# The first loads of an attention and gated-MLP kernel: heads on even and odd rows, whole weight units, and the masks' second part on another queue

## The chip, the cores and the metric

The kernel runs on one core of a Trainium2 chip. The metric is the time of one execution on the device, in microseconds (us). It was measured in three runs before the change: 947.91, 950.3 and 950.68 us, with a median of 950.3 us.

## The reference

The program computes windowed attention and puts its output through a gated MLP. All is in float32, for 8 batches, 8 heads, 576 positions and 64 numbers a head.

```
rel = pos[:, None] - pos[None, :]
mask = rel in [0, 32)                       for heads 0 to 3
mask = rel in [0, 128) and rel % 4 == 0     for heads 4 to 7
s = where(mask, q @ k.T / 8, -1e9)          # per batch and head
x = softmax(s) @ v                          # laid out as (4608 tokens, 512)
g = x @ w_gate                              # (512, 1536)
out = (silu(g) * (x @ w_val)) @ w_out       # (4608, 512)
```

A query sees 32 keys at most, in neighbouring positions or in every fourth one.

## The kernel before

**Packs.** Attention goes in packs: a pack holds two heads and up to a few groups of 128 queries. A group is four blocks of 32 queries, and each block sees 64 keys, so the scores of a block are a product of 32 columns of q with 64 columns of k. The first four packs (0 to 3) make the first 512 tokens of x and have four groups each; they have code of their own (`first_...`). Here the two heads of a pack are done by one product: the 128 rows hold head 0 in 64 of them and head 1 in the other 64, k stands twice, once for each head with zeros in the other head's rows, and so the product gives both heads side by side. The same goes for v.

**Weights.** The MLP's weights come in 24 units of 128 rows and 768 KB (two units for each of the 12 columns of 128 hidden numbers), as 64-bit floats. A unit is converted in five steps, named by the letters E, T, B, H, L: E (L242) on ScalarE, T on ScalarE (L259) or VectorE (L262), B (L269 or L272) on VectorE, H (the high part, L280) on ScalarE and L (the low part, L284) on GpSimd. Raw units stand in six places at first; a place comes free after step B, and then the next unit is loaded (`w_load`, L229 once `ready["w"]` is set).

**The order at the start.** All loads are issued on three queues: that of SyncE (SP), that of ScalarE (ACT), and that of GpSimd (POOL), each in order. `first_qk(m)` and `first_v(m)` load a pack's q and k, and v, as two halves: rows 0 to 63 (head 0) on the sync queue, rows 64 to 127 (head 1) on GpSimd's. The zeros that go with them are written by VectorE or GpSimd. A weight unit before `ready["w"]` also comes as two halves of 64 rows on these two queues (L231, L232). The masks' first part (128 x 640 of bf16) comes at the very start on ScalarE's queue, and the second part (128 x 320 of bf16, 80 KB), which pack 4 is the first to read, on the sync queue after five weight units (L607). A wait is there where a load's semaphore is still in use: there are eight for the loads that SP and ACT issue and eight for GpSimd's, given out in turn, so a load waits until the one eight before it has landed.

After the loads a written order follows, kept for TensorE, VectorE and ScalarE by `manual_schedule`:

```
for what in ("Q0 S0 Q1 Y2 S1 X0 Q2 X1 T0 S2 T1 K0 K1 A0 X2 N0 W0 T2 W1 A1 K2 W2 U0 Q3 H0 N1 W3 S3 U1 W4 A2 H1 "
             "L1 X3 N2 W0 T3 K3 W1 U2 A3 H2 L0 W2 W0 N3 W3 W4 W1 W0 U3 H3 L2 W1 W2 W0 L3 W2 W3 W1").split():
```

The digit is the pack. Q are the scores on TensorE (a mask product L372, then 32 small products L376), S the maximum and the subtraction on VectorE (L383, L384), X the exp on ScalarE (L440), T the transposition (L444) and K its copy (L450), A the product with v (L392), N the division by the sums on VectorE (L399 to L401), U the transposition back (L478), H and L the high and low part of x (L505 on ScalarE, L508 on VectorE). W0 to W4 are the steps E, T, B, H, L of the next weight unit.

**After it.** Then come the MLP's columns: `gv_mm` makes a column's gate and value products (bg and bv, L518, 12 products each), `act_tanh` (L527) and `dve_u` (L532) read the gate's bank, and only then can the next column's gate product write it; `out_mm` (L555) makes the output product of the column before. The attention of the later packs is put in between (`attend`): pack 4's mask products (L414) and scores (L420) come first. What isn't in the written order is placed by the scheduler, which may put a later product ahead of waiting ones, and each engine then keeps that order.

Of the kernel before, what the change touches and what calls it, by code (L numbers as in the profile page):

```python
# [12 lines left out]
I32 = mybir.dt.int32  # L13
# [5 lines left out]
P = 128  # L19
# [120 lines left out]
def attention_moe(ctx, tc, qkb, vb, w, masks, ident, out):  # L140
# [76 lines left out]
    def w_load():  # L217
        nonlocal loaded
        u = loaded
        n = u % 6 if u < NU - NLAST else (u + 2) % 4  # L220

        if u >= NU or raw_of.get(n, -1) >= done["B"]:
            return False
        raw_of[n] = u
        loaded += 1
        t = at(raw_at[n], 2 * WU, I32)
        src = w[u // 2, u % 2].bitcast(I32)
        if ready["w"]:
            last["w"] = nc.sync.dma_start(out=t, in_=src)  # L229
        else:  # L230
            nc.sync.dma_start(out=t[:D], in_=src[:D])  # L231
# [116 lines left out]

    def first_qk(m, zero):

        t, n = early["qk"](), pk(m).cols
        k = n - FN
        nc.sync.dma_start(out=t[:D, :n], in_=qkb[m, :D, :n])
        nc.gpsimd.dma_start(out=t[D:, k:k + n], in_=qkb[m, D:, :n])
        zero.memset(t[D:, :k], 0.0)
        zero.memset(t[:D, n:n + k], 0.0)
        st[m]["qk"] = t

    def first_v(m, zero):
# [5 lines left out]
        zero.memset(t[:D, 1], 0.0)  # L365
        st[m]["v"] = t.rearrange("p h (g c) -> p h g c", c=D + 1)

    def first_scores(m, bank):
        t, n = st[m]["qk"], pk(m).cols
        kk = t[:, :2 * n].rearrange("p (h c) -> p h c", h=2)  # L370
        mk = masks_of(m).rearrange("q (g k) -> q g k", g=FG).unsqueeze(2).broadcast_to([P, FG, 2, BK])
        nc.tensor.matmul(out=bank.rearrange("q (g h k) -> q g h k", g=FG, h=2), lhsT=ident16, rhs=mk, start=True,  # L372
                         stop=False, skip_group_check=True)
        for g, blocks in enumerate(pk(m).groups):
            for j, (_, _, _, q, k) in enumerate(blocks):
                nc.tensor.matmul(out=bank[BQ * j:BQ * j + BQ, P * g:P * g + P], lhsT=t[:, n - FN + q:n - FN + q + BQ],  # L376
                                 rhs=kk[:, :, k - FN:k - FN + BK], start=False, stop=g == FG - 1,
                                 skip_group_check=True)

    def first_shift(m, bank):  # L380
        mx, e = early["bm"](2 * FG), early["e"]()
        s, ev = [x.rearrange("q (g k) -> q g k", k=BK) for x in (bank, e)]
        nc.vector.reduce_max(out=mx, in_=s, axis=mybir.AxisListType.X)  # L383
        nc.vector.tensor_tensor(out=ev, in0=s, in1=mx.unsqueeze(2).broadcast_to([P, 2 * FG, BK]), op=ALU.subtract)  # L384
        st[m]["e"] = e.rearrange("q (g h k) -> q g h k", g=FG, h=2)

# [37 lines left out]
    def shift(m, two, pool, masked):  # L424
# [10 lines left out]
        nc.vector.tensor_tensor(out=ev, in0=s, in1=mx.unsqueeze(3).broadcast_to([P, 2, ng, BK]), op=ALU.subtract)  # L435
        st[m]["e"] = e

# [4 lines left out]
    def turn_e(m, bank):  # L442
        for g in range(pk(m).ng):
            nc.tensor.transpose(out=bank[:, P * g:P * g + P],  # L444
                                in_=st[m]["e"][:, g].rearrange("q h k -> q (h k)"), identity=idents[:, 0])

# [133 lines left out]
    near = P + 8 * BK  # L580
    nc.vector.memset(ones, 1.0)
    nc.vector.memset(some, 0.0)
    first_qk(0, nc.vector)
    nc.scalar.dma_start(out=consts[:, :near], in_=masks[:, :near])
    first_qk(1, nc.vector)
    nc.sync.dma_start(out=idents, in_=ident.rearrange("n p c -> p n c"))
    nc.scalar.activation(out=some, in_=some, func=AF.Exp)

    warm = ones.bitcast(BF16)
# [5 lines left out]

    idle(WARM)
    first_qk(2, nc.gpsimd)
    first_v(0, nc.vector)
    w_load()
    first_v(1, nc.gpsimd)  # L600
    first_qk(3, nc.gpsimd)
    first_v(2, nc.gpsimd)
    w_load()
    first_v(3, nc.gpsimd)
    for _ in range(3):
        w_load()
    nc.sync.dma_start(out=consts[:, near:], in_=masks[:, near:])  # L607
    while w_load():
        pass
    ready["w"] = True  # L610
# [10 lines left out]

    et = mybir.EngineType
    with tc.manual_schedule(engines={et.PE, et.DVE, et.Activation}):
        for what in ("Q0 S0 Q1 Y2 S1 X0 Q2 X1 T0 S2 T1 K0 K1 A0 X2 N0 W0 T2 W1 A1 K2 W2 U0 Q3 H0 N1 W3 S3 U1 W4 A2 H1 "
# [360 lines left out]
def layout(q, k, v, moe_w_gate, moe_w_val, moe_w_out):  # L985
# [3 lines left out]
    for m, pk in enumerate(PACKS):  # L989
        for i, (b, q0, n, qc, kc) in enumerate(x for g in pk.groups for x in g):  # L990
# [3 lines left out]
            for j in range(2):  # L994
                h, r = 2 * pk.pair + j, D * j
                nq = P * pk.ng
                x, y = (pk.cols - nq, -nq) if m < 4 and j == 0 else (0, 0)
                qkb[m, r:r + D, x + qc:x + qc + n] = q[b, h, qt].T
                qkb[m, r:r + D, y + kc + a:y + kc + e] = k[b, h, kt[a:e]].T
                vb[m, r + a:r + e, i, :D] = v[b, h, kt[a:e]]  # L1000
# [28 lines left out]
```

## Time and profile before

| | |
|---|---|
| median of three runs | 950.3 us |
| the profiled execution | 949.9 us |
| its span, first to last instruction | 948.1 us |
| TensorE busy | 926.8 us (98%) |
| VectorE, ScalarE, GpSimd busy | 641.0, 390.6, 256.8 us |
| mean granted TensorE clock | 0.996 |
| DMA, mean over the span | 217 GB/s |

The profiled execution is one of its own. Its span leaves out 1.8 us around the instructions. In the tables below a row of the chain of work is a start, a length and what the time went to; a row of the timeline is a start, a busy time, an engine, a line, an operation with what it writes and reads, and in brackets the idle time before it with what ended it; a row of windows has busy times of PE, PEld, DVE, ACT and POOL, then the granted clock, the DMA engines' busy share and their GB/s.

### The profile page before, as it was taken

To read this page: it belongs to the slowest core of one execution; us is meant where nothing else is said; L and a number is where in the kernel's file an instruction comes from. 1 tells how busy PE (TensorE), PEld (TensorE's weight loads), DVE (VectorE), ACT (ScalarE), POOL (GpSimd) and SP (SyncE) were. 2 spreads that over 40 slices of the span, in tenths; PEclk is the share of its full clock that TensorE was granted. 3 is DMA by queue.
4 is the path that set the end of the run, shared out by engine and by line. 5 is a ranking of instruction groups with operands and counts; after the bars stand their busy time and mean duration, and the time that the engine had idled before them with its cause. 6 is when DMAs were issued, how large, how long until landed. Compare 5 with 4: busy or idle time off the path is not lost.

```text
span 948.1 us, 20559 instructions
## 1 busy us (share of the span) xinstructions
PE 926.8 (98%) x8499; PEld 755.1 (80%) x8499; DVE 641.0 (68%) x1055; ACT 390.6 (41%) x664; POOL 256.8 (27%) x313
## 2 busy tenths in 40 slices
PE   7699999999999989999999999999999999999998
PEld 4587888878888878888888888888888888888886
DVE  5665755777687776466668975576689845656863
ACT  3566642333243333334335553334345623334351
POOL 7265441111111121122222211222222122333320
PEclk9899999999999999999999999999999999999999
DMA  9986522777676892576776768676766686556663
GB/s 256 315 285 215 169 82 92 241 239 253 218 267 236 270 331 80 177 236 216 222 240 219 244 227 273 204 250 201 245 209 199 203 264 198 187 192 200 190 212 109
DMA packets 75181, 205.45 MB, mean 217 GB/s; under 512 B 7760, under 2 KB 22352, under 8 KB 75088
## 3 DMA queue, kind: packets, MB, share of 16 engines
q0 software_dynamic: 28336, 103.66, 35.3%
q1 hardware_dynamic: 34656, 62.36, 19.2%
q10 hardware_dynamic: 12096, 38.12, 11.7%
q8 instruction: 67, 1.10, 0.5%
q14 instruction: 26, 0.21, 0.1%
HBM read 161.64 MB, written 42.47 MB: 215 GB/s over the span
## 4 chain that ended last, share of the span: by engine, by line
PE 92%; DMA 4%; DVE 2%; ACT 1%; issue 1%; SPq 0%; DVEq 0%; ACTq 0%
PE bo L843 31%; PE bv L843 12%; PE bg L843 12%; PE bg L518 10%; PE bo L555 10%; PE bv L518 9%; PE two L460 3%; PE two L420 3%; DMA at_bfloat<-masks 2%; PE two L444 1%; DMA at_float<-vb 1%; PE two L478 1%; ACT at_float L527 0%; DVE at_float L532 0%; DVE at_float32r L492 0%
## 5 line engine op out<-in xcount | busy, mean ns | idle before, releaser
L843 PE MATMUL bo<-at_float32r 128*128 128x512 f32 x1296 | 307.1, 390 | 0.0
L843 PEld LDWEIGHTS bo<-at_float32r 128*128 128x128 f32 x1296 | 242.2, 188 | 50.7
L772 POOL DMA_DIRECT2D at_float32r<-pieces x189 | 101.7, 538 | 377.1 <-PE bo L843 216.6
L806 DVE TENSOR_TENSOR at_float<-bo,at_float 128x512 f32<-128x512 f32 (+1 forms) x169 | 114.2, 684 | 105.2 <-ACT at_float L848 49.7
L806 DVE TENSOR_TENSOR at_float32r<-at_float,at_float32r 128x512 fp32r<-128x512 f32 (+1 forms) x147 | 114.0, 800 | 42.2 <-ACT at_float32r L833 27.2
L843 PE MATMUL bv<-at_float32r 128*128 128x512 f32 x486 | 129.7, 393 | 0.0
L843 PE MATMUL bg<-at_float32r 128*128 128x512 f32 x486 | 129.4, 392 | 0.0
L518 PE MATMUL bg<-at_float32r,at_float32r 128*128 128x512 f32 x432 | 108.3, 398 | 2.3 <-ACT at_float32r L280 1.2
L518 PE MATMUL bv<-at_float32r,at_float32r 128*128 128x512 f32 x432 | 108.1, 397 | 0.0
L555 PE MATMUL bo<-at_float32r,at_float32r 128*128 128x512 f32 x432 | 106.3, 394 | 0.0
L843 PEld LDWEIGHTS bv<-at_float32r 128*128 128x128 f32 x486 | 90.2, 188 | 19.2
L843 PEld LDWEIGHTS bg<-at_float32r 128*128 128x128 f32 x486 | 90.3, 188 | 18.9
L547 POOL TENSOR_TENSOR at_float32r<-at_float,at_float32r 128x512 fp32r<-128x512 f32 x36 | 49.1, 1364 | 207.0 <-PE bo L555 146.3
L833 ACT CAST at_float32r<-at_float 128x512 fp32r<-128x512 f32 x126 | 76.9, 622 | 68.0 <-PE bv L843 21.4
L518 PEld LDWEIGHTS bg<-at_float32r,at_float32r 128*128 128x128 f32 x432 | 81.0, 190 | 21.0 <-DVE at_float L532 2.0
L518 PEld LDWEIGHTS bv<-at_float32r,at_float32r 128*128 128x128 f32 x432 | 80.5, 189 | 17.2
L555 PEld LDWEIGHTS bo<-at_float32r,at_float32r 128*128 128x128 f32 x432 | 79.7, 188 | 17.0
L869 ACT ACTIVATE at_float<-at_float 128x512 f32<-128x512 f32 x72 | 45.6, 633 | 81.4 <-DVE at_float L806 81.3
L848 ACT COPY at_float<-bg 128x512 f32<-128x512 f32 x63 | 37.0, 587 | 94.1 <-PE bg L843 93.9
L532 DVE SCALAR_TENSOR_TENSOR at_float<-at_float,bg 128x512 f32<-128x512 f32 x36 | 24.7, 687 | 70.0 <-ACT at_float L527 70.0
L284 POOL TENSOR_TENSOR at_float32r<-at_int,at_float32r 128x768 fp32r<-128x768 f32 x24 | 43.4, 1817 | 54.4 <-ACT at_float32r L280 54.4
L871 DVE SCALAR_TENSOR_TENSOR at_float<-at_float,at_float 128x512 f32<-128x512 f32 x72 | 49.4, 686 | 10.7 <-ACT at_float L869 10.6
(99 smaller groups left out, 924.8 us busy)
## 6 DMA issues: line engine op xcount, KB each, us to landing
at_float32r<-pieces POOLq DMA_DIRECT2D x189, 512.0 KB, 3.7
pieces<-at_float32r SPq DMA_DIRECT2D x126, 256.0 KB, 3.3
at_int<-w SPq DMA_DIRECT2D x18, 768.0 KB, 5.7
out<-at_float SPq DMA_DIRECT2D x35, 256.0 KB, 4.1
at_float<-vb ACTq DMA_DIRECT2D x15, 520.0 KB, 5.4
at_float<-vb ACTq DMA_DIRECT2D x20, 390.0 KB, 4.8
at_float<-qkb ACTq DMA_DIRECT2D x13, 544.0 KB, 5.8
at_float<-qkb ACTq DMA_DIRECT2D x12, 448.0 KB, 5.3
```

The lines of the kernel that those rows point to most:

```text
L284: nc.gpsimd.tensor_tensor(out=lo, in0=wst.pop(u).bitcast(F32), in1=hi, op=ALU.subtract)
L420: nc.tensor.matmul(out=two[BQ * j:BQ * j + BQ, h, a + BK * g:a + BK * g + BK], lhsT=t[r, q:q + BQ], rhs=t[r, k:k + BK], start=not masked, ...
L518: nc.tensor.matmul(out=bank[:, :CH], lhsT=wcol(f, o, low), rhs=x[ORDER[j]], start=n == 0, stop=n == len(ops) - 1)
L547: nc.gpsimd.tensor_tensor(out=hl, in0=hst[i][0], in1=hst[i][1], op=ALU.subtract)
L555: nc.tensor.matmul(out=bank_o[j][:, :CH], lhsT=wcol(f, 2 * DM + P * j, low), rhs=x, start=f == 0 and low == 0 and x is hh, stop=f == NF - ...
L772: nc.gpsimd.dma_start(out=taken[asked], in_=pieces[asked % NPIECE])
L806: engine.tensor_tensor(out=out, in0=a, in1=b, op=op)
L833: nc.scalar.copy(out=o[:, 0], in_=src)
L843: nc.tensor.matmul(out=bank, lhsT=w, rhs=x, start=first and n == 0 and t in FRESH, stop=last and n == len(ops) - 1, skip_group_check=True)
L848: nc.scalar.copy(out=kept[KEPT[t]][r], in_=banks[0][r][:, :CS])
L869: nc.scalar.activation(out=f, in_=g, func=AF.Tanh, scale=0.5)
L871: nc.vector.scalar_tensor_tensor(out=f, in0=f, scalar=1.0, in1=g, op0=ALU.add, op1=ALU.mult)
```

## The change

`first_qk` now makes three loads and not two: q of both heads in one load of 128 rows (2 KB each), then k of head 0 to the even rows and k of head 1 to the odd ones, 64 rows each. In front of each of the two it writes zeros over all 128 rows of that part. `first_v` does the same for v: head 0 on even and head 1 on odd rows, zeros over all rows first. The subtraction in `first_shift` writes its result with the two heads interleaved, key by key, so that the transposition gives rows in the same order. The host lays q out in that order of rows.

A weight unit is always loaded by one load of 128 rows on the sync queue. The masks' second part is loaded on ScalarE's queue, right after the small exp that loads ScalarE's table, and ahead of the third pack. The first loads stand in a `manual_schedule` for SP, POOL, DVE and ACT, and GpSimd's instructions of the written order are kept in that order too.

```
 def w_load():
-        if ready["w"]:
-            last["w"] = nc.sync.dma_start(out=t, in_=src)
-        else:
-            nc.sync.dma_start(out=t[:D], in_=src[:D])
-            nc.gpsimd.dma_start(out=t[D:], in_=src[D:])
+        last["w"] = nc.sync.dma_start(out=t, in_=w[u // 2, u % 2].bitcast(I32))
...
-    def first_qk(m, zero):
+    def first_qk(m, *zero):
         t, n = early["qk"](), pk(m).cols
         k = n - FN
-        nc.sync.dma_start(out=t[:D, :n], in_=qkb[m, :D, :n])
-        nc.gpsimd.dma_start(out=t[D:, k:k + n], in_=qkb[m, D:, :n])
-        zero.memset(t[D:, :k], 0.0)
-        zero.memset(t[:D, n:n + k], 0.0)
-        st[m]["qk"] = t
+        tk = t[:, FN:FN + 2 * k].rearrange("p (h c) -> p h c", h=2)
+        nc.sync.dma_start(out=t[:, :FN], in_=qkb[m, :, :FN])
+        for h in range(2):
+            zero[h].memset(tk[:, h], 0.0)
+            (nc.sync, nc.gpsimd)[h].dma_start(out=tk[h::2, h], in_=qkb[m, D * h:D * h + D, FN:n])
+        st[m]["qk"] = t[:, :FN], tk
...
 def first_v(m, *zero):
-        nc.sync.dma_start(out=t[:D, 0], in_=vb[m, :D, :n])
-        nc.gpsimd.dma_start(out=t[D:, 1], in_=vb[m, D:, :n])
-        zero.memset(t[D:, 0], 0.0)
-        zero.memset(t[:D, 1], 0.0)
+        for h in range(2):
+            zero[h].memset(t[:, h], 0.0)
+            (nc.sync, nc.gpsimd)[h].dma_start(out=t[h::2, h], in_=vb[m, D * h:D * h + D, :n])
...
 def first_shift(m, bank):
-        nc.vector.tensor_tensor(out=ev, in0=s, in1=mx.unsqueeze(2).broadcast_to([P, 2 * FG, BK]), op=ALU.subtract)
-        st[m]["e"] = e.rearrange("q (g h k) -> q g h k", g=FG, h=2)
+        nc.vector.tensor_tensor(out=e.rearrange("q (g k h) -> q g h k", g=FG, h=2),
+                                in0=bank.rearrange("q (g h k) -> q g h k", g=FG, h=2),
+                                in1=mx.rearrange("q (g h) -> q g h", h=2).unsqueeze(3).broadcast_to([P, FG, 2, BK]),
+                                op=ALU.subtract)
+        st[m]["e"] = e.rearrange("q (g c) -> q g c", g=FG)
...
+    with tc.manual_schedule(engines={et.SP, et.Pool, et.DVE, et.Activation}):
+        nc.vector.memset(ones, 1.0)
+        nc.vector.memset(some, 0.0)
+        first_qk(0, nc.vector, nc.gpsimd)
+        nc.scalar.dma_start(out=consts[:, :near], in_=masks[:, :near])
+        first_qk(1, nc.vector, nc.gpsimd)
+        nc.sync.dma_start(out=idents, in_=ident.rearrange("n p c -> p n c"))
+        nc.scalar.activation(out=some, in_=some, func=AF.Exp)
+        nc.scalar.dma_start(out=consts[:, near:], in_=masks[:, near:])
+        idle(WARM)
+        first_qk(2, nc.vector, nc.gpsimd)
+        first_v(0, nc.vector, nc.gpsimd)
         w_load()
+        first_v(1, nc.vector, nc.gpsimd)
+        first_qk(3, nc.gpsimd, nc.gpsimd)
+        first_v(2, nc.vector, nc.gpsimd)
+        w_load()
+        first_v(3, nc.gpsimd, nc.gpsimd)
+        for _ in range(3):
+            w_load()
+        while w_load():
+            pass
...
-    with tc.manual_schedule(engines={et.PE, et.DVE, et.Activation}):
+    with tc.manual_schedule(engines={et.PE, et.DVE, et.Activation, et.Pool}):
...
+                rq = slice(j, P, 2) if m < 4 else slice(r, r + D)
+                qkb[m, rq, qc:qc + n] = q[b, h, qt].T
+                qkb[m, r:r + D, kc + a:kc + e] = k[b, h, kt[a:e]].T
```

More of the change, by code (lines that the diff above doesn't have):

```diff
@@ L375, in first_scores @@
             for j, (_, _, _, q, k) in enumerate(blocks):
-                nc.tensor.matmul(out=bank[BQ * j:BQ * j + BQ, P * g:P * g + P], lhsT=t[:, n - FN + q:n - FN + q + BQ],
+                nc.tensor.matmul(out=bank[BQ * j:BQ * j + BQ, P * g:P * g + P], lhsT=t[:, q:q + BQ],
                                  rhs=kk[:, :, k - FN:k - FN + BK], start=False, stop=g == FG - 1,
@@ L381, in first_shift @@
         mx, e = early["bm"](2 * FG), early["e"]()
-        s, ev = [x.rearrange("q (g k) -> q g k", k=BK) for x in (bank, e)]
+        s = bank.rearrange("q (g k) -> q g k", k=BK)
         nc.vector.reduce_max(out=mx, in_=s, axis=mybir.AxisListType.X)
-        nc.vector.tensor_tensor(out=ev, in0=s, in1=mx.unsqueeze(2).broadcast_to([P, 2 * FG, BK]), op=ALU.subtract)
-        st[m]["e"] = e.rearrange("q (g h k) -> q g h k", g=FG, h=2)
+        nc.vector.tensor_tensor(out=e.rearrange("q (g k h) -> q g h k", g=FG, h=2),
[3 more added lines that the diff above has]
+        st[m]["e"] = e.rearrange("q (g c) -> q g c", g=FG)
     def first_results(m, two):
@@ L435, in shift @@
         nc.vector.tensor_tensor(out=ev, in0=s, in1=mx.unsqueeze(3).broadcast_to([P, 2, ng, BK]), op=ALU.subtract)
-        st[m]["e"] = e
+        st[m]["e"] = e.rearrange("q g h k -> q g (h k)")
     def exps(m):
@@ L444, in turn_e @@
             nc.tensor.transpose(out=bank[:, P * g:P * g + P],
[L445 removed]
+                                in_=st[m]["e"][:, g], identity=idents[:, 0])
     def keys(m, bank, pool):
@@ L580, in attention_moe @@
     near = P + 8 * BK
[L581 to L587, printed above, removed]
+    et = mybir.EngineType
     warm = ones.bitcast(BF16)
@@ L594, in idle @@
                              rhs=warm.unsqueeze(1).broadcast_to([P, 4, P]), start=True, stop=True)
[L596 to L605, printed above, removed]
-        w_load()
-    nc.sync.dma_start(out=consts[:, near:], in_=masks[:, near:])
-    while w_load():
-        pass
+    with tc.manual_schedule(engines={et.SP, et.Pool, et.DVE, et.Activation}):
[10 more added lines that the diff above has]
+        first_v(0, nc.vector, nc.gpsimd)
+        w_load()
+        first_v(1, nc.vector, nc.gpsimd)
[7 more added lines that the diff above has]
+            pass
     ready["w"] = True
@@ L995, in layout @@
                 h, r = 2 * pk.pair + j, D * j
[L996 to L999, printed above, removed]
+                rq = slice(j, P, 2) if m < 4 else slice(r, r + D)
+                qkb[m, rq, qc:qc + n] = q[b, h, qt].T
+                qkb[m, r:r + D, kc + a:kc + e] = k[b, h, kt[a:e]].T
                 vb[m, r + a:r + e, i, :D] = v[b, h, kt[a:e]]
```

7 lines of the change are left out of this document (2 added, 5 removed).

## The prediction

> **What bounds the kernel now.** I read the page first, for where the engines are not full. Of the 40 slices only the first two show TensorE below 9, and in the same slices the DMA engines are at 9 throughout.
>
> ```profile
> span 948.1 us, 20559 instructions
> PE   7699999999999989999999999999999999999998
> DMA  9986522777676892576776768676766686556663
> ```
>
> After the second slice TensorE is the bound, and nothing in the diff touches that part. So what the change is worth is how much sooner TensorE gets into its unbroken run. The chain of work that ended last, cut to the first 60 us, shows where that run begins and what came before it.
>
> ```profile
> 3.78 0.61 SPq L231
> ...
> 4.44 13.44 DMA at_float<-vb
> ...
> 17.90 19.90 DMA at_bfloat<-masks
> ...
> 37.84 0.61 PE two L414 x2
> 38.45 0.43 PE bv L518
> ...
> 41.33 0.94 PE bg L518 x4
> ...
> 42.29 0.61 ACT at_float L527
> ...
> 42.92 0.70 DVE at_float L532
> ...
> 43.67 3.02 PE bg L518 x12
> ```
>
> Read backwards: the gate product of the second weight column starts at 43.67 and from there TensorE is never idle for long; it waited for the bank that tanh (L527) and the next step (L532) read, and the first column's products could not end before 42.27 (41.33 + 0.94), because in TensorE's queue they stood behind the mask product L414, which waited for the second part of the masks. That load was issued at 17.90, since the sync queue waited for a load of v, and it landed at 37.80. The list of waits has the price on TensorE:
>
> ```profile
> PE two L414 <- DMA at_bfloat<-masks: 5.4, 1, 5.4
> PE bg L518 <- ACT at_float32r L280: 1.2, 1, 1.2
> ```
>
> The second question is what would be late next. Two answers of the DMA view, for 2 to 36 us and for 40 to 46 us:
>
> ```profile
> DMA packets 2723, 9.37 MB, mean 276 GB/s; under 512 B 477, under 2 KB 946, under 8 KB 2721
> at_int<-w SPq DMA_DIRECT2D x6, 384.0 KB, 18.4
> at_float<-vb SPq DMA_DIRECT2D x4, 260.0 KB, 15.0
> at_float<-qkb SPq DMA_DIRECT2D x1, 288.0 KB, 8.9
> ...
> DMA packets 473, 2.49 MB, mean 416 GB/s; under 512 B 48, under 2 KB 48, under 8 KB 473
> ```
>
> The engines are full in both, but move 276 GB/s while every load is two halves of 64 rows on two queues, and 416 GB/s while units of 128 rows go whole over one queue. A packet costs more in the first stretch; it isn't the number of bytes. And ScalarE waits for these loads again and again (L242 is the first step of each weight unit):
>
> ```profile
> 14.40 0.65 ACT L440 ACTIVATE at_float<-at_float 128x512 f32<-128x512 f32 x1
> 16.23 0.88 ACT L242 ACTIVATE at_int<-at_int 128x768 f32<-128x768 f32 x1 [1.18 <-DMA at_int<-w]
> ...
> 32.64 0.91 ACT L242 ACTIVATE at_int<-at_int 128x768 f32<-128x768 f32 x1 [1.14 <-DMA at_int<-w]
> ```
>
> So the start is bound by the rate of the loads, and at its end by one small load that stood last in a full queue.
>
> **The change, part by part.** *Masks early.* The load (80 KB) moves from behind four weight units on the sync queue to ScalarE's queue at about 3 us; ScalarE has nothing else to do until its first exp, so the issue is free. It delays the loads behind it by 80 KB, 0.2 us at 416 GB/s. TensorE's wait of 5.4 us goes. Late next are the products that wait for the fourth pack (below).
>
> *Whole rows.* A load's rows now lie over all 128 rows: weight units and q as 128 rows, keys and v on every second row. For units the row of 416 GB/s is the same transfer. For every-second-row loads the trace has none; I bound the stage's rate by 276 (nothing gained) and 416, and take 360, nearer the upper end: more than half the bytes (weights and q) are of the kind that ran at 416. [...]
>
> *The ladder to 43.67.* I go up from the first scores.
>
> ```profile
> 0.00:5.00 5.00, 3.99 (x10) 1.35 (x10) 3.19 (x7) 1.49 (x2) 3.84 (x11) 1.00 0.64 172
> ...
> 6.89 1.93 PE L376 MATMUL fs<-at_float 128*32 128x128 f32 x32 [1.44 <-DVE at_float L365]
> 17.90 0.96 DVE L269 SCALAR_TENSOR_TENSOR at_int<-at_int 128x768 int32<-128x768 int32 x1 [1.53 <-ACT at_int L259]
> 29.26 0.17 DVE L399 TENSOR_SCALAR at_float<-fr 128x8 f32<-128x8 f32 x1 [0.56 <-PE fr L392]
> 29.70 0.69 DVE L401 TENSOR_TENSOR at_float<-fr,at_float 128x512 f32<-128x512 f32 x1
> 34.04 0.69 DVE L508 TENSOR_TENSOR at_float32r<-fs,at_float32r 128x512 fp32r<-128x512 f32 x1
> ...
> L383 DVE TENSOR_REDUCE at_float<-fs 128x8 f32<-128x512 f32 x4 | 2.8, 692 | 6.1 <-PE fs L376 6.1
> L384 DVE TENSOR_TENSOR at_float<-fs,at_float 128x512 f32<-128x512 f32 x4 | 2.8, 692 | 0.1
> L262 DVE TENSOR_SCALAR at_int<-at_int 128x768 int32<-128x768 int32 x2 | 1.9, 954 | 1.0 <-ACT at_int L242 1.0
> ```
>
> 1. The first scores start at 6.89, when the halves of pack 0 are in. They now need q0, two key parts of 160 KB and the masks' first part; with what is issued beside them some 0.75 MB. The first 5 us move 172 GB/s × 5 us = 0.86 MB, so I put them at 5.0, 1.9 earlier.
> 2. From there to the end of the third exp (14.40 + 0.65) it is compute and keeps its 8.2 us: 13.2.
> 3. Then ScalarE takes weight unit 0, if it is in. Ahead of its end lie 3.68 MB: q0 to q2 and three packs' keys 1680 KB, masks and identities 368, three halves of v 780, the unit 768. At 360 GB/s it is in at 5 + (3.68 − 0.86)/0.36 = 12.8, so just no wait (345 is the limit). Its start to the end of L269 is 16.23 to 18.86 now, 2.6: 15.8.
> 4. From there VectorE's written order sets the pace: three norms of 1.13 each (29.26 to 30.39), one shift (2 × 0.69 + 0.04 = 1.42), four low parts of x (0.68), two shifts of weights (0.95) and two joins (0.96): 3.39 + 1.42 + 2.72 + 1.91 + 1.92 = 11.4, with twelve gaps of 0.05 some 12.0. The fourth pack's low part (L508) then ends at 27.8, where it now ends at 34.73. The loads must keep up: now it ends 2.1 after unit 3 is read at 32.62. Unit 3 has 7.91 MB up to its end and is in at 5 + 7.05/0.36 = 24.6 and needed at 25.7; 340 GB/s is the limit, at 276 it is in at 30.5 and the low part ends at 32.6.
> 5. The first column's gate product ends after that. Now 11 products ran from 38.45 to 42.27, 3.8 us, at these clocks:
>
> ```profile
> 27.40:30.80 3.40, 3.40 (x36) 2.72 (x36) 2.36 (x5) 0.93 (x2) 0.00 (x0) 0.50 1.02 282
> 30.80:37.60 6.80, 1.67 (x9) 1.06 (x8) 5.67 (x6) 4.62 (x7) 1.82 (x2) 1.00 1.03 245
> 37.70:41.00 3.30, 3.16 (x9) 2.52 (x10) 0.06 (x1) 0.47 (x1) 3.24 (x2) 0.50 1.00 324
> 43.70:52.00 8.30, 8.30 (x36) 6.64 (x36) 5.62 (x6) 6.64 (x10) 4.85 (x3) 1.00 0.87 341
> ```
>
>    The clock was half for 3.3 us after TensorE had been busy for 1.67 of 6.8 us. At full clock 36 products take 8.3 us, so 11 take 2.5. I take 3.1 between the two: 30.9. [...]
> 6. Tanh and the next step keep their 1.4 (42.27 to 43.67): 32.3. I add 0.9 for products that the scheduler puts ahead of ready work, as the 1.2 of L518 behind L280 in the list of waits: 33.2.
>
> Gain: 43.7 − 33.2 = 10.5 us.
>
> *Costs.* Zeros now lie under the loads, so each key or v load waits for its memset:
>
> ```profile
> 0.84 0.11 DVE L581 MEMSET at_float<- 128x64 f32 x1 [0.84 <-PEq L1021]
> 1.16 0.59 DVE L355 MEMSET at_float<- 64x640 f32 x1 [0.20 <-issue]
> 7.74 0.51 POOL L354 DMA_DIRECT2D at_float<-qkb  x1
> 13.90 0.96 POOL L365 MEMSET at_float<- 64x1040 f32 x1
> 37.51 3.43 POOL L284 TENSOR_TENSOR at_float32r<-at_int,at_float32r 128x768 fp32r<-128x768 f32 x2 [4.21 <-ACT at_float32r L280]
> ```
>
> A memset goes by columns, so 128 rows cost what 64 did. On VectorE the first ends at 1.75, and six (three of up to 0.59, three of v at up to 0.96, with gaps of 0.2) end by 7, ahead of its first work on scores. The sync queue issues nine loads up to and with unit 0 where it issued six, at 0.61 each (3.78, L231), so unit 0 is asked for at about 6.5 us and not at 3.8; by 7 the engines, at 0.86 MB in 5 us and 0.28 a us after, have moved 1.4 MB of the 2.9 that stand before the unit: no starving. The one new wait that reaches far is v of pack 3: its memset is GpSimd's, behind seven of its loads (0.51 each) and nine memsets (four of v at 0.96, five of keys at about 0.6), at 0.84 + 3.6 + 6.8 = 11.2; on the sync queue units 2 to 5 stand behind it, and ScalarE's L242 waits for those. So zero: by 11.2 at 360 GB/s 3.1 MB are moved of the 5.8 up to unit 1's end, so 2.7 MB or 7.5 us of work lie in the queue; if GpSimd were later than that, each us more would appear in step 4. GpSimd loses six unit halves (3.1 us), hidden either way. The shift's subtraction (L384) now writes every second element: L242 works in place on every second element at 0.88/768 = 1.15 ns an element, no slower than L384's 692/512 = 1.35 on plain ones, so 0 taken; twice its time would put 0.7 on step 4 and 0.7 on step 2.
>
> **The sum.** 948.1 − 10.5 = 937.6 for the span; the profiled run had 949.9 with 1.8 around it, so 939.4, and the median of 950.3 stands 0.4 above that run: 939.8, said as 940.
>
> **The rivals.** *The rate stays at 276 GB/s*, because the engines or their small packets and not the rows set it, or every-second-row loads drag. Against it: the 416. Then only the masks' wait goes: 32.6 + 3.1 + 1.4 + 0.9 = 38.0, gain 5.7, 945.
>
> *A new wait in the first steps.* TensorE comes to the second and third column earlier than units 2 to 4, or the load of pack 4, which waits for a buffer and five units. Now unit 2's low part is done at 39.2 (37.51 and half of 3.43), 4.5 before 43.67. By my ladder unit 4 is read near 26.5 (8.7 MB at 360 GB/s), after that ScalarE writes unit 2's high part, and its low part is done at 26.5 + 2 × 0.9 + 1.7 = 30.0, 3 before 33.2. Price 3 us: 943.
>
> *Slower: every-second-row loads are slow.* The place is the same ladder. Keys and v are 3.34 MB of the 7.91 before unit 3. For 2.8 us more than now the second column must start at 46.5, so unit 3 must land at 39; with the other 4.57 MB at 416 (11 us, from 2 us on) that leaves 26 us for 3.34 MB: it decides from 128 GB/s down, about half of the lowest stretch (245). Then 953 or more. Against it: each of the sixteen DMA engines would have to move 4 KB rows at half the pace that it now has in halves.
>
> **Chances and range.** Forecast 0.62, rate stays 0.25, new wait 0.08, slow rows 0.05. The range goes from 936 (0.75 MB are moved by 4.4 in step 1, no gaps in step 4, full clock in step 5, no slip in step 6: 0.6 + 0.6 + 0.6 + 0.9 less, 937.1, rounded down) to 946 (the first rival with 0.7 for the clock, 945.3, rounded up). A difference of 0.3%, 2.8 us, is about what can be told from none. All but the last case lie beyond it; some of the second and third could shrink into it: faster 0.92, same 0.04, slower 0.04.
>
> **What would show it.** L414 with no DMA wait; some 340 to 415 GB/s from 10 to 25 us, where the rows of now have 276 for the mean; L242 of units 0 and 3 without a wait; the last L508 of the start near 28 and the second gate product near 33. It is wrong if the rate stays below 340, if VectorE has idle time in step 4 that neither loads nor TensorE explain, or if TensorE's idle time comes back between 33 and 100 us.

## The result and the profile after

The changed kernel takes 935.14 us (median of 4 runs, 934.47 to 937.22) beside 949.66 us for the kernel before (4 runs, 947.91 to 950.68). The ratio is 0.9853, with a 95% interval from 0.983 to 0.9875. Forecast were 940.0 us and a range from 936 to 946: the sign was right, and the gain, 14.5 us by the medians, is larger than the range allowed. The profiled execution took 934.96 us, with a span of 933.2, so 14.9 less than the 948.1 of before.

The page of the profile after, the same rows as of before:

```profile
span 933.2 us, 20559 instructions
PE   7999999999999999999999999999999999999998
DMA  9974515667786980767777778766766686656663
```

At the start only the first slice is now below 9 for TensorE. The 8 of the fifteenth slice of before (332 to 356 us) is gone too; what it was is told below. The DMA engines are full for two slices as before, and then at 7 in the third where they were at 8: the same loads are done sooner. The DMA view of the changed kernel, for 2 to 36 us and then for 10 to 24 us:

```profile
DMA packets 3841, 13.20 MB, mean 388 GB/s; under 512 B 538, under 2 KB 1050, under 8 KB 3838
...
DMA packets 1439, 5.77 MB, mean 412 GB/s; under 512 B 222, under 2 KB 222, under 8 KB 1437
```

In the same 34 us the engines moved 13.20 MB where they had moved 9.37, at 388 GB/s and not 276; in the part in which they are never short of work, at 412. The timeline of the changed kernel has the rungs of the ladder (columns as before; L370 are the scores, L237 step E, L264 step B, L505 the low part of x, L515 the gate product, L524 tanh):

```profile
6.63 1.08 PE L370 MATMUL fs<-at_float 128*32 128x128 f32 x32 [1.19 <-DMA at_float<-qkb]
13.77 1.00 ACT L237 ACTIVATE at_int<-at_int 128x768 f32<-128x768 f32 x1
15.82 0.95 DVE L264 SCALAR_TENSOR_TENSOR at_int<-at_int 128x768 int32<-128x768 int32 x1
25.83 0.94 ACT L237 ACTIVATE at_int<-at_int 128x768 f32<-128x768 f32 x1 [0.49 <-DMA at_int<-w]
26.52 0.40 PE L411 MATMUL two<-at_bfloat 128*128 128x256 bf16 x2
27.90 0.68 DVE L505 TENSOR_TENSOR at_float32r<-fs,at_float32r 128x512 fp32r<-128x512 f32 x1
28.63 1.41 PE L515 MATMUL bg<-at_float32r,at_float32r 128*128 128x512 f32 x5 [0.41 <-DVE at_float32r L505]
30.22 0.59 ACT L524 ACTIVATE at_float<-bg 128x512 f32<-128x512 f32 x1
31.58 3.02 PE L515 MATMUL bg<-at_float32r,at_float32r 128*128 128x512 f32 x12 [0.41 <-DVE at_float L529]
```

The mask product (L411) no longer waits. Behind the fourth low part only five gate products are left. The second column's gate product starts at 31.58 where it started at 43.67: 12.1 us of the 14.9 are won by then. The list of waits on TensorE of the changed kernel begins so:

```profile
PE fs L370 <- DMA at_float<-qkb: 1.2, 1, 1.2
PE fr L389 <- POOL at_float L359: 1.1, 1, 1.1
PE two L457 <- DVE at_float32r L489: 1.1, 3, 0.4
```

Nothing above 1.2 us is left. The first scores still wait for their keys, since key loads now stand behind memsets. The second row is the first product with v: it starts 0.25 us after the second half of the first v has landed (13.37), as it does in runs 7 and 11 (12.54 and 12.92), so it waits for that load, and the memset that the row names was only GpSimd's last event before.

The other 2.8 us come later. I lined up the same products of both traces: the lead is 11.8 us at 80 us (times of before), 12.2 at 340, 13.1 at 345, 14.3 at 350, 14.7 at 930 and 14.9 at the end. So 2.1 us come between 343 and 350 us, in a place that the change doesn't touch. The lists of waits for 330 to 360 us of the kernel before, and the same wait in the list of the changed kernel:

```profile
PE two L444 <- ACT at_float L440: 1.9, 1, 1.9
PE bg L518 <- DVE at_float L532: 0.6, 1, 0.6
```

```profile
PE two L441 <- ACT at_float L437: 0.7, 1, 0.7
```

L444 and L441 are the same line. Experiments 9 to 11 are about this.

### The profile page after: what moved, and what is told of

Read it like the earlier page. It is cut to its first block, busy times and chain, and to the rows that moved or that the text cites. A ratio compares the mean times of both kernels' runs of the same rounds, so it can differ in the third digit from the quotient of the medians.

```text
span 933.2 us, 20559 instructions
## 1 busy us (share of the span) xinstructions
PE 921.8 (99%) x8499; PEld 751.5 (81%) x8499; DVE 639.2 (68%) x1055; ACT 391.1 (42%) x664; POOL 253.8 (27%) x307
## 3 DMA queue, kind: packets, MB, share of 16 engines
q10 hardware_dynamic: 12240, 38.20, 11.9%
## 4 chain that ended last, share of the span: by engine, by line
PE 73%; DVE 3%; DMA 1%; issue 1%; ACT 1%; SPq 0%; ACTq 0%; DVEq 0%
PE bo L841 32%; PE bv L841 12%; PE bg L841 12%; PE bo L552 4%; PE bg L515 4%; PE bv L515 4%; PE two L457 2%; PE two L417 2%; DMA pieces<-at_float32r 1%; PE two L441 1%; PE two L475 1%; DVE at_float32r L732 0%; SPq L740 0%; DVE at_float L529 0%; DVE at_float L719 0%
## 5 line engine op out<-in xcount | busy, mean ns | idle before, releaser
L804 DVE TENSOR_TENSOR at_float32r<-at_float,at_float32r 128x512 fp32r<-128x512 f32 (+1 forms) x147 | 114.0, 800 | 40.0 <-ACT at_float32r L831 27.1
L515 PE MATMUL bg<-at_float32r,at_float32r 128*128 128x512 f32 x432 | 106.7, 394 | 0.8 <-DVE at_float32r L505 0.4
L515 PE MATMUL bv<-at_float32r,at_float32r 128*128 128x512 f32 x432 | 107.1, 394 | 0.0
L515 PEld LDWEIGHTS bg<-at_float32r,at_float32r 128*128 128x128 f32 x432 | 79.9, 188 | 18.8 <-DVE at_float32r L505 1.2
L515 PEld LDWEIGHTS bv<-at_float32r,at_float32r 128*128 128x128 f32 x432 | 79.7, 188 | 17.1 <-DVE at_float L534 0.4
L869 DVE SCALAR_TENSOR_TENSOR at_float<-at_float,at_float 128x512 f32<-128x512 f32 x72 | 49.4, 686 | 10.7 <-ACT at_float L867 10.6
```

Of the source, the lines that this page charges most:

```text
L515: nc.tensor.matmul(out=bank[:, :CH], lhsT=wcol(f, o, low), rhs=x[ORDER[j]], start=n == 0, stop=n == len(ops) - 1)
L804: engine.tensor_tensor(out=out, in0=a, in1=b, op=op)
L869: nc.vector.scalar_tensor_tensor(out=f, in0=f, scalar=1.0, in1=g, op0=ALU.add, op1=ALU.mult)
```

## The experiments

Each kernel is the kernel before or the changed one with a small edit. "Second column" is the start of the gate product that stood at 43.67 before and at 31.58 after; the rate is the mean over 2 to 36 us. That start is read from one profile of each kernel, and it differs between executions: 43.52 to 44.80 in three profiles of the kernel before, 31.34 and 31.58 in two of the changed one. So differences of about 1 us in this column say nothing.

| run | from | median us | ratio to before, 95% | second column | GB/s |
|---|---|---|---|---|---|
| 1 masks early | before | 946.35 | 0.997, 0.9958 to 0.9981 | 39.79 | 280 |
| 2 units whole | before | 945.51 | 0.9966, 0.9954 to 0.9977 | 41.54 | 281 |
| 3 units in halves, two queues | after | 954.19 | 1.0067, 1.0051 to 1.0082 | 49.85 | 267 |
| 4 masks late | after | 936.1 | 0.9871, 0.9854 to 0.9887 | 31.68 | 389 |
| 5 units in even and odd rows | before | 943.88 | 0.9947, 0.9932 to 0.9962 | 39.83 | 319 |
| 6 units in halves, one queue | after | 946.36 | 0.9975, 0.9964 to 0.9985 | 40.16 | 269 |
| 7 units in even and odd rows, one queue | after | 937.91 | 0.9884, 0.987 to 0.9899 | 31.87 | 388 |
| 8 keys and v in halves | after | 944.35 | 0.9948, 0.9931 to 0.9965 | 40.84 | 283 |
| 11 changed kernel again | after | 935.02 | 0.9865, 0.9847 to 0.9884 | 31.34 | 393 |
| 12 zeros of the first v by VectorE | after | 935.08 | 0.9863, 0.9848 to 0.9878 | 31.81 | 387 |

The question is which part of the change brings the 12.1 us: the masks, the number of queues and loads, or the rows that a load covers. The fixed order of the first loads and of GpSimd was not tried alone; runs 6 and 8 keep it, with the masks early, and their second column starts 2.8 to 3.5 us sooner than before, where the masks alone (run 1) bring 3.9. So it shows no gain of its own.

### 1: the masks' part alone

```
+    nc.scalar.dma_start(out=consts[:, near:], in_=masks[:, near:])      # behind the small exp
...
-    nc.sync.dma_start(out=consts[:, near:], in_=masks[:, near:])
```

> The kernel before with one edit: the masks' second part is loaded on ScalarE's queue at the start. Theory (the rate of the loads and the masks' wait are two limits, one behind the other): the loads keep their 276 GB/s, the low part of x for the fourth pack still ends near 34.7, L414 does not wait, and the second column's gate product starts near 39.5 in place of 43.7: 4 us faster, 945.5. Rival (the masks' wait alone held the start, the rate is hidden behind it): nearly all of the 12 us by which the second column starts sooner in the changed kernel, 938 or less. Other rival (another wait takes its place): under 1.5 us faster.

The second column starts 3.9 us sooner and the kernel is 3.0 us faster by the medians. The mask product runs at 32.92 and waits for nothing, but the list of waits has a new first row:

```profile
PE fr L392 <- DMA at_float<-vb: 3.6, 1, 3.6
```

The rate stays at 280 GB/s, and the loads come as late as before or up to 1.5 us later. So without faster loads the masks are worth 3 to 4 us; the prediction's first rival, in which only this wait goes, had 5.7.

### 2: whole units alone

```
-            nc.sync.dma_start(out=t[:D], in_=src[:D])
-            nc.gpsimd.dma_start(out=t[D:], in_=src[D:])
+        last["w"] = nc.sync.dma_start(out=t, in_=w[u // 2, u % 2].bitcast(I32))
```

> The kernel before with one edit: each weight unit is one load of 128 rows on the sync queue; q, k and v stay in halves of 64 rows on two queues, the masks' second part stays late. Theory (rows set the rate): units move near 400 GB/s and halves near 276, unit 3 is in near 28 in place of 32.6, the masks, behind five units on the sync queue, land near 32, and the second column starts near 38: 5 to 6 us faster, 944.5. Rival (the number of queues or GpSimd's half of the work sets the rate, not the rows): with units on one queue the rate falls or stays at 276, the masks land near 38 or later, no gain or a loss of 1 to 3 us.

Only 2.1 us at the second column, where 5 to 6 were expected. By the medians the kernel is 3.9 us faster; the profiled execution (947.32 us) is the slowest of its nine. The first wait of its list, and the 40 slices of GB/s for 2 to 36 us (0.85 us each):

```profile
PE fr L387 <- DMA at_float<-vb: 6.1, 1, 6.1
```

```profile
GB/s 354 211 195 297 292 258 225 221 217 202 254 293 261 243 245 272 280 226 225 228 243 251 285 276 220 227 246 332 151 211 217 337 398 369 439 390 394 429 395 430
```

The engines move some 400 GB/s from the 32nd slice (28.4 us) on, when all halves of q, k and v but one are through; before that, with whole units and halves side by side, the engines move mostly 200 to 300. Besides, a whole unit now stands on the sync queue ahead of v. So in this run units of 128 rows came to some 400 GB/s only when the loads of half the rows were nearly all through.

### 8: keys and v back in halves

The complement of 2: the changed kernel, whole units, and each key and v load on rows 0 to 63 or 64 to 127.

```
-            (nc.sync, nc.gpsimd)[h].dma_start(out=tk[h::2, h], ...)
+            (nc.sync, nc.gpsimd)[h].dma_start(out=tk[D * h:D * h + D, h], ...)      # the same for v
...
-        nc.vector.tensor_tensor(out=e.rearrange("q (g k h) -> q g h k", g=FG, h=2),
+        nc.vector.tensor_tensor(out=e.rearrange("q (g h k) -> q g h k", g=FG, h=2),
```

> The changed kernel, but head 0 of k and v in rows 0 to 63 and head 1 in rows 64 to 127 (q laid out to match, the shift's result not interleaved); zeros over all rows, whole units and the masks stay as changed. Theory (rows): k and v, 3.3 MB of the first 7.9, move at 270 and not 400 GB/s; v of packs 1 to 3 and unit 3 land 3 to 4 us later, the second column starts near 34: 2.5 us slower than the changed kernel, 937.5. Rival (the interleaved write of the shift costs VectorE what the rows gain, or the loads of k and v are hidden): within 0.5 us or faster.

9.3 us are lost at the second column, far more than expected. The windows for 10 to 24 and 24 to 36 us (PE, PEld, DVE, ACT, POOL busy, granted clock, DMA share, GB/s), and the first wait:

```profile
10.00:24.00 14.00, 8.39 (x136) 6.02 (x139) 5.78 (x10) 4.97 (x8) 4.39 (x6) 0.86 1.05 252
24.00:36.00 12.00, 11.01 (x146) 7.39 (x138) 9.02 (x18) 7.27 (x11) 3.06 (x2) 0.88 1.02 347
```

```profile
PE fr L389 <- DMA at_float<-vb: 5.1, 1, 5.1
```

Queues, their order and the number of loads are those of the changed kernel; only rows differ (and the place of the shift's result, which takes 0.69 us either way), and the rate in 10 to 24 us falls from 412 to 252. The engines are full in both (a share of 1.05 here, 1.02 in the changed kernel). So each of the two parts needs the other, and taking one away costs most of the gain.

### 6 and 3: units back in halves

In 6 both halves go on the sync queue, in the place of the whole unit; in 3 the second half goes on GpSimd's, as before.

```
-        last["w"] = nc.sync.dma_start(out=t, in_=w[u // 2, u % 2].bitcast(I32))
+            nc.sync.dma_start(out=t[:D], in_=src[:D])
+            last["w"] = nc.sync.dma_start(out=t[D:], in_=src[D:])      # 3: nc.gpsimd.dma_start(out=t[D:], in_=src[D:])
```

> The changed kernel, but the first six weight units come as rows 0 to 63 and then rows 64 to 127, both on the sync queue. Unlike the run with halves on two queues, no other instruction changes place in SP's or GpSimd's order. Theory (rows): a half alone on the queue moves at 200 to 280 GB/s, unit 3 lands near 28 to 30 in place of 25.8, the second column starts 2 to 4 us later than in the changed kernel: 938. Rival (the split over two queues was at fault): within 0.5 us of the changed kernel, 935.

> The changed kernel with one part undone: weight units before the first free buffer come again as rows 0 to 63 on the sync queue and rows 64 to 127 on GpSimd's. q, k, v and masks as in the changed kernel. Theory (rows set the rate): the rate falls to near 276 GB/s while units move; unit 3 is in near 29 in place of 25.8, the fourth pack's low part ends near 31.5 in place of 28.6, the second column starts near 34.5 in place of 31.6: 3 us slower than the changed kernel, 938. Rival (the loads are no longer a limit at all once the masks are early): within 0.5 us of the changed kernel.

Run 6: 8.6 us later than the changed kernel at the second column. Its window has halves one after another on one queue:

```profile
24.00:36.00 12.00, 7.92 (x58) 5.44 (x58) 8.07 (x12) 5.49 (x8) 1.73 (x1) 0.86 1.03 238
```

238 GB/s with the engines full (1.03): two loads of 384 KB land 1.65 us apart. Run 3 was 16 us off its expectation, and not for its rate alone (229 GB/s for 24 to 36 us): the order in the queues changed with the edit. The low part L284 came ahead of pack 3's v on GpSimd, and a later unit's load, which must wait for step B, ahead of it on the sync queue. The first waits on TensorE and GpSimd:

```profile
PE fr L394 <- DMA at_float<-vb: 8.3, 2, 6.1
```

```profile
POOL at_float32r L284 <- ACT at_float32r L280: 7.7, 1, 7.7
```

So run 3's time tells nothing on the price of halves over two queues, and 6 stands for it. But its rate tells something: from 24 to 36 us halves of units run on both queues, beside some loads of v and one whole unit, and the engines, shown full, move no more than on one queue in run 6:

```profile
24.00:36.00 12.00, 4.87 (x51) 3.17 (x49) 4.93 (x9) 3.19 (x5) 3.56 (x6) 0.88 1.03 229
```

### 5 and 7: rows or queues

In 5 the kernel before gets units in even and odd rows, on the same two queues in the same order; in 7 the changed kernel does, both on the sync queue. A load has 64 rows in both, as in 6.

```
-            nc.sync.dma_start(out=t[:D], in_=src[:D])
-            nc.gpsimd.dma_start(out=t[D:], in_=src[D:])
+            nc.sync.dma_start(out=t[0::2], in_=src[0::2])
+            nc.gpsimd.dma_start(out=t[1::2], in_=src[1::2])      # 7: nc.sync
```

> The kernel before with one edit: the two halves of a weight unit, on the same two queues and in the same places of them, take the even and the odd rows and not rows 0 to 63 and 64 to 127. Nothing else, and no order, changes. Theory (the rows that a load covers set the rate): units move near 400 GB/s, q, k and v in their halves near 270, 0.33 over both; the masks' second part lands near 30 and not at 37.8, the second column starts near 36: 7 us faster, 942. Rival (two queues, or GpSimd as the issuer, set the rate): 276 GB/s as before, within 1 us of the kernel before.

> As the run with halves on one queue, but the two loads of a unit take the even and the odd rows. Theory (rows): about 410 GB/s as with whole units, within 0.5 us of the changed kernel, 935. Rival (a load of 64 rows is slow however its rows lie): 2 to 4 us slower, as with rows 0 to 63 and 64 to 127.

The windows of run 5, for 10 to 24 us (units mixed with halves of q, k and v) and for 30 to 36 us (units alone), and of run 7 for 24 to 36 us:

```profile
10.00:24.00 14.00, 11.07 (x186) 7.33 (x185) 7.50 (x14) 6.31 (x10) 8.61 (x11) 1.00 1.03 294
...
30.00:36.00 6.00, 3.23 (x13) 2.34 (x13) 5.58 (x7) 5.12 (x7) 2.98 (x2) 0.82 1.03 416
```

```profile
24.00:36.00 12.00, 10.31 (x46) 7.26 (x45) 8.96 (x13) 8.04 (x12) 7.61 (x5) 1.00 1.01 406
```

64 rows that lie over all 128 moved at 406 to 416 GB/s, on one queue or on two; in run 7 two loads of 384 KB land 0.95 us apart (up to 28.9 us, whole units after that). 64 rows side by side moved at 238 on one queue; on two, at 266 to 307 in three profiles of the kernel before (10 to 24 and 24 to 36 us) and at 229 in run 3. Between runs 6 and 7 only the rows differ, with the same number and size of loads on the same queue. That settles it for these loads: the rows set the rate, 238 for halves one after another against 406 for every second row. What makes neighbouring rows slower, no run shows.

Run 5 gains 3.8 us at the second column. It keeps the masks' wait (2.7 us for L414), and 294 GB/s while halves of q, k and v are in flight. Run 7 has the changed kernel's rate and start (31.87), but its time misses the theory of 935: it is 1.8 to 2.9 us slower, by its ratio to the kernel before against those of the changed kernel (0.9865 and 0.9853). Of the 3.2 us between the spans 1.4 are lost by 80 us, at the exp of pack 4 (L446 waits 1.2 us; why is open), 0.9 at 343 to 350 us and most of the rest by hundredths; both of these also differ between executions of one kernel (below).

### 4: masks late again

```
-        nc.scalar.dma_start(out=consts[:, near:], in_=masks[:, near:])
...
+        nc.sync.dma_start(out=consts[:, near:], in_=masks[:, near:])      # behind five units
```

> The changed kernel with one part undone: the masks' second part is again on the sync queue behind five weight units. Theory: the queue now empties at 413 GB/s, so the masks land near 29 and not 37.8; the mask product stands in TensorE's queue at 26.5, so it waits some 2.5 us, and the products behind it, of which the last could start at 28.6 anyway, lose 1 to 2 us: 936.5. Rival (the place of the load alone is worth the 5.4 us that TensorE waited in the kernel before): 940.

The second column starts at 31.68, 0.1 later. With loads at 389 GB/s the masks land at 27.1, and the mask product, which the scheduler now puts at 31.14, waits for nothing, against the theory. So the 5.4 us of waiting that the prediction read from the chain are worth 3 to 4 us alone and nothing next to fast loads, at the second column: the parts do not add up.

### 9, 10 and 11: both kernels again

The text is unchanged; these are fresh profiles, for the 2.1 us at 340.

> The kernel before once more, nothing changed, for a second profile of it. At 340 to 350 us the first profile of it has waits of 1.9 us (L444 for the exp, L440) and 0.6 us (L518 for L532); the profiles of the eight other kernels gained 0.8 to 2.1 us against it just there, whatever they changed at the start. Theory (these waits differ from one execution to the next, with the time that the stores to pieces take): 0.5 to 1.5 us less waiting there, span near 947.0. Rival (they belong to the kernel before, by something that its start leaves behind): again 1.9 and 0.6, span 948.1.

> The kernel before a third time, for a third profile. Theory: the waits of L444 and L518 at 340 to 350 us differ again from both profiles by some tenths to 1.5 us, span 946.5 to 948.5. Rival: 1.9 and 0.6 as in the first, span within 0.2 of 948.1.

> The changed kernel once more, nothing changed, with more runs of both kernels. Its start must repeat: second column's gate product at 31.6, 12.1 earlier than before. Theory (draw): against the first profile of before it gains 0.8 to 2.1 us at 340 to 350 us and not always 2.1; the median over more runs comes to 12 to 14 us under that of before. Rival (belongs to the kernel): again 2.1 there and 14.5 us by the medians.

The two fresh profiles of before have spans of 945.6 and 946.1 us, and against the first they gain 2.4 to 2.5 us each at 343 to 350. There the wait of L444 is 0.4 us in both, where the third was expected to differ again (the row of the second):

```profile
PE two L444 <- ACT at_float L440: 0.4, 1, 0.4
```

Behind it stands ScalarE's copy of mixed weights (L731, L729 after), which waits until the stores of the last ones to memory have landed. That copy in the first profile, in the second, and in the changed kernel:

```profile
340.56 1.05 ACT L731 CAST at_float32r<-at_float 128x1024 fp32r<-128x1024 f32 x1 [5.34 <-DMA pieces<-at_float32r]
```

```profile
338.06 1.05 ACT L731 CAST at_float32r<-at_float 128x1024 fp32r<-128x1024 f32 x1 [2.98 <-DMA pieces<-at_float32r]
```

```profile
326.26 1.05 ACT L729 CAST at_float32r<-at_float 128x1024 fp32r<-128x1024 f32 x1 [3.21 <-DMA pieces<-at_float32r]
```

The four stores ahead of it, by issues and median time to landing, in the same order:

```profile
pieces<-at_float32r SPq DMA_DIRECT2D x4, 256.0 KB, 6.2
```

```profile
pieces<-at_float32r SPq DMA_DIRECT2D x4, 256.0 KB, 4.8
```

```profile
pieces<-at_float32r SPq DMA_DIRECT2D x4, 256.0 KB, 4.6
```

So the stores landed late by chance in the execution from which the prediction was made: 6.2 us, where the third profile of before has 4.7 and run 11 has 5.4 (it asked for them 0.8 us sooner than the first profile of after, and the last of them landed at the same 325.83). What delayed them is open. The rival falls: the wait does not belong to the kernel before. It is the first profile that stands out, for the other thirteen of this document all gain on it there, by 0.8 to 2.5 us. From profile to profile with 945.6 or 946.1 for before, the changed kernel (933.2, and 933.2 again in run 11) gains 12.4 to 12.9 us. At the second column, at 43.52 and 44.80 in these two, the changed kernel's first profile is 11.9 and 13.2 us ahead, so the gain comes from the start in both. In run 11 the second column starts 0.24 us sooner than in the first profile of after, but the copy starts at 326.26 again and the span is the same: at this place stores, ScalarE and VectorE make the chain, and a small lead of TensorE is lost there. The kernel before took 947.83 us in the runs beside 11 (7 runs, 946.23 to 949.48), so between medians the gain is 12.8 there and 14.5 in the first comparison; with the two profiles I take 12.5 to 14.5 for what the change brings.

### 12: the next wait

```
-        first_v(0, nc.vector, nc.gpsimd)
+        first_v(0, nc.vector, nc.vector)
...                                      # and masks late, as in 4, so run 4 is the kernel to compare with
```

> The changed kernel with two edits: VectorE writes both zero parts of the first v (GpSimd wrote the second, and its load could only be issued at 6.55), and the masks' second part goes on the sync queue after the first units as in e4. Theory (from 15.8 to 28.6 VectorE's written order is the bound, and it starts when v of pack 0 is in): GpSimd's loads from the first v on are issued 1.1 us earlier, the first products with v start at 12.7 and not at 13.62, the last low part (L505) ends 0.3 to 0.7 earlier and the second column's gate product starts at 30.9 to 31.3; in all 934.5, not to be told from the changed kernel by times. Rival (the loads are the bound, since unit 3 lands at 25.8 whatever the order): 31.6 and no gain.

No gain: 935.08 us, second column at 31.81 (31.68 in run 4). The second half of the first v landed at 11.71 (13.37 in the changed kernel, 13.03 in run 4), as meant. But the scores cost more. The timeline and the windows of this kernel, and then the same row of run 4:

```profile
6.92 1.54 PE L370 MATMUL fs<-at_float 128*32 128x128 f32 x32 [2.13 <-POOL at_float L359]
```

```profile
7.40:10.80 3.40, 3.40 (x58) 2.10 (x46) 1.39 (x2) 0.63 (x1) 2.89 (x5) 0.50 1.03 406
```

```profile
6.57 1.93 PE L370 MATMUL fs<-at_float 128*32 128x128 f32 x32 [1.12 <-DMA at_float<-qkb]
```

TensorE waited for 2.1 us ahead of the first scores (for their keys, which landed at 6.8; the memset that the row names was only the last event before), and then the clock was half for 3.4 us (0.50 from 7.40 to 10.80); in the changed kernel it waited for 1.2 and ran at full clock, 1.08 us for the scores. The length of the wait does not decide this alone: run 4 waited for 1.1 us and its scores took 1.93 us, run 1 waited for 1.7 and they took 1.08. That the 1.93 us were at half the clock is an estimate, from the 1.08: the windows of run 4 have 1.00 from 5 to 10 us. What sets the clock, the runs do not show. The third exp ended at 14.93 and not at 13.67 (14.75 in run 4), which took what v had gained. Of the theories, the rival's outcome came, but not its reason: unit 3 landed at 24.80 (25.80 in the changed kernel), so the loads did not hold the start. VectorE's written order, with its waits for TensorE, did from its second norm on: from there to the end of the fourth low part it took 11.3 us in the changed kernel (from 17.26), in run 4 (17.34) and here (17.50). Ahead of it there was slack: the first norm waited for 1.0 us in runs 4 and 12 and for 1.9 in the changed kernel, so exps that ended 1.1 to 1.3 us later cost 0.1 to 0.2 at the second column.

## Why the prediction was right or wrong

Right was the cause; wrong were sizes in the sum. The terms that failed are step 5 with the slip of step 6 (4.0 us taken, where 1.6 were measured and no slip), and the base of 948.1 us, which held 2.1 to 2.5 us of chance. Whole rows lift the rate to where loads no longer set the end, and most of the named signs are there: L411 (L414) without a DMA wait, 412 GB/s in 10 to 24 us within 340 to 415, unit 0 without a wait, the last L505 at 27.90 to 28.58. One is not: unit 3 was waited for, 0.49 us. The rival that the rate stays is refuted by 412, where the same stretch of before had 289, and every second row is not slow (416 and 406 GB/s in runs 5 and 7).

Step by step, predicted and measured:

| step | predicted | measured |
|---|---|---|
| 1 first scores start | 5.0 | 6.63 |
| 2 third exp ends | 13.2 | 13.67 |
| 3 unit 0 is in; its step B ends | 12.8; 15.8 | 13.74; 16.77 |
| 4 fourth low part ends; unit 3 is in | 27.8; 24.6 | 28.58; 25.80 |
| 5 first column's gate product ends (tanh starts) | 30.9 | 30.22 |
| 6 second column's gate product starts | 33.2 | 31.58 |

*Step 1* was 1.6 us too early. The working took the bytes by the mean rate of the first 5 us, and some 0.8 MB were indeed moved by then; but they were shared with loads issued behind the keys, and when the keys were in, at 6.3 and 6.5, 1.37 MB had been moved and not 0.75. Besides, the keys could be asked for at 1.65 only, behind their memsets, which the prediction had put at nothing; what each of the two cost was not tried. *Step 2* gave most of it back: 7.0 us and not 8.2, since the scores ran at full clock (1.08 us, where they had taken 1.93). That was not foreseen, and it was luck: run 4's scores took 1.93 us after a wait of like length. It also mattered little, as runs 4 and 12 show, with the exps later and the second column 0.1 to 0.2 us later. *Step 4* came out right, 11.8 us and not 12.0 from the end of step B to the end of the fourth low part, but in part by luck: VectorE waited for TensorE for 0.49 us (for v of pack 1, in at 15.86) and for 0.69 us, where gaps of 0.6 in all were allowed, and the rest took 10.6 us and not 11.4, since an instruction that followed at once started some 0.08 us before the listed end of the one before (21.02 after 20.42 + 0.68). The interleaved write of L378 takes 0.69 us as L384 did. Unit 3 came 1.2 later than said, though the rate was higher, because loads started later: unit 0 was in at 13.74 and not at 12.8. ScalarE waited 0.49 us for unit 3, hidden.

*Steps 5 and 6* are where the gain of the start was mis-sized. Eleven products at 3.1 us were taken from the row of before; with the fourth low part as the only thing late, all but five had been done in the gaps before it, and these took 1.41 us at full clock, 1.6 with the wait. And the 0.9 us for products put ahead of ready work did not come: from tanh's start to the next gate product it is 1.4 us, as in the working without the slip. Together that is 2.4 us too much, against 0.8 us too little up to step 4: 33.2 for 31.58, a gain of 12.1 and not 10.5. No run shows the 0.7 us for the clock in the upper end of the range, the 3.8 us of the profile of before less the 3.1 taken; in its place the changed kernel's five products took their 1.41 us at full clock.

The rest of the miss is the base. The prediction said that nothing in the diff touches what comes after the start, which is so, but it subtracted from a profile that held 2.1 to 2.5 us of chance at 343 to 350 us: it took one profile for the kernel. Its own first view had the trace of it: it says that only the first two of the 40 slices are below 9, but the fifteenth (332 to 356 us) and the last are at 8. By the two fresh ones (945.6 and 946.1) the same steps would have given 935.1 or 935.6 for the span and 937 for the time, in the range's lower part; the range left out that the kernel before scatters: its medians in four sets of runs were 947.83, 948.73, 949.38 and 949.66 us. Another 0.7 us of the lead grow by hundredths between 80 and 800 us; run 10, an unchanged kernel, shows the same growth against the first profile, and run 9 shows none, so they are not the change's. Of the 4.4 us between the span forecast, 937.6, and 933.2 the start has 1.6, the place at 343 to 350 us 2.1 and this growth 0.7.

GpSimd's chain was longer than worked out: it issued v of pack 3 at 14.79 and not at 11.2. The working had left out one memset of v (five stand before that load, 0.96 us each) and the 0.3 us that each of eight loads waited for its memset; with these 3.4 us it comes to 14.6. The cover that the prediction named held, since work was queued for the DMA engines all the time.

Three smaller readings of the prediction were off without changing its sum. "A packet costs more in the first stretch" does not follow from the two rows that it shows: they have 80 and 79 packets a microsecond (2723 in 34 us, 473 in 6 us), with 3.4 and 5.3 KB each, so they left open that small packets set the rate. It is true of packets of one size (6 KB: 356 ns in the median from 2 to 36 us, 238 from 40 to 46), and the changed kernel settles it: the mean packet has 3.4 KB again, and 113 a microsecond are moved (3841 in 34 us). Unit 4 comes to 26.8 by the stated rate, not 26.5 (it landed at 27.69). And the masks stood behind five units, not four.

## What to carry to other kernels

Let every load of a busy stretch cover rows over all 128 partitions: two heads or tables that need 64 rows each go on even and odd rows (406 to 416 GB/s here), and not on the lower and upper half (229 to 307). Change all of the loads of that stretch at once, because here one kind that stayed in halves held the others back (249 to 252 GB/s, where all together had 412). Before a gain is subtracted from one profile, look for waits on DMA landings in it, and take a second profile of the unchanged kernel. And ask of each term of a chain what fills the time before it: products that had to wait in one profile may be done in the gaps of the next.

## What the runs showed of the hardware

Loads of 64 neighbouring rows slowed whole loads that were in flight with them. With whole units and halves mixed the engines moved 249 to 252 GB/s (runs 2 and 8, 10 to 24 us) while showing themselves full, where whole loads and loads of every second row together moved 412. The packets show it too: the profile records these transfers in pieces, and for a unit a piece has 6 KB. The medians:

| loads | run | ns for a packet of 6 KB |
|---|---|---|
| whole rows, or every second row | changed kernel and 7, 10 to 36 us | 234 to 238 |
| halves on two queues | before, 9 and 10, 10 to 36 us | 314 to 375 |
| halves on one queue | 6, 24 to 36 us | 415 |
| halves on two queues | 3, 24 to 36 and 38 to 46 us | 476 and 420 |
| whole units beside halves of k and v | 2 and 8, 10 to 24 us | 391 and 375 |

What a second queue brings to halves is not settled: 266 to 307 GB/s in three profiles of the kernel before against 238 on one queue, so 12 to 29% more, but 229 in run 3. In no run is it twice as much.

A memset of 128 rows took the time of one of 64: 0.93 us for 1040 columns on VectorE in both kernels, 0.63 us for 640 on GpSimd.

The first scores took different times in kernels whose TensorE had waited alike: 1.93 us after 1.1 us in run 4, 1.08 us after 1.2 in the changed kernel and after 1.7 in run 1. And the time from issue to landing of the same four stores went from 4.6 to 6.2 us between executions, at a place where it moves the whole kernel by up to 2.5 us.
